# Splitting the second layer's weight slices in a staggered order, and moving conversions and the permutation into the experts

## The chip, the core and the metric

The kernel runs on one core of a Trainium2 chip. Its engines are TensorE (PE; its weight loads are a row of their own, PEld), VectorE (DVE), ScalarE (ACT), GpSimd (POOL) and SyncE (SP), which issues most DMAs. The metric is the device time of one execution in microseconds, a median over runs.

## What is computed

Attention with two sparse masks feeds a mixture of eight experts, one expert per token, and that feeds a second feed-forward layer on all tokens. Cut to what matters here:

```python
x = attention(q, k, v)                       # 2304 tokens of 512
expert_idx = argmax(logits(x, expert_emb))   # one of 8 experts per token
for e in range(8):                           # F = 1024
    h = np.maximum(x[mask] @ w1[e], 0.0)
    out[mask] = gate_w[mask, None] * (h @ w2[e])
h = np.maximum(np.maximum(x @ v1, x @ v2), x @ v3)   # second layer, 768 wide
return h @ v_out
```

All of it is in float32. The kernel keeps that precision by splitting each operand into a rounded high half and the rest (a low half), and multiplies high by high, high by low and low by high: three matmuls for one (`three`, line 818).

## The kernel before

**Stages.** Attention comes first (to some 112 us), then routing, then the experts in order of size (112 to 353 us), then the second layer in three blocks of 768 tokens. In each block `layer1` runs over nine weight slices (numbers 64 to 72) and `layer2` over six groups of 128 tokens.

**Weight slices.** Slices 0 to 63 are the experts' weights, eight for each expert: four for the first product (`gemm1`, two steps f for each slice) and four for the second (`gemm2`, steps d). In the code's tables a step is a pair (e, i): i is f for 0 to 7 and 8 + d after that. Slices 64 to 72 (`UP`) are the second layer's first weights, 73 to 75 its last. A slice is loaded by `w_load` (line 120) into one of three staging tiles, then split by three functions that `w_stages` (line 141) returns: `sums` (line 157, only for `UP`: four VectorE operations that form the combined blocks of the product scheme below, in a small tile `sb`), `upper` (line 162: the high half, on ScalarE, L166) and `rest` (line 168: the low half, on VectorE, L171, then for `UP` the store to `u_scr` for the later blocks, then the next `w_load`). The halves go into a ring of nine tiles; an `UP` slice takes two of them. `freed` (line 191) says which of the ring may be written.

**The planner.** Nothing is scheduled by the compiler: each engine runs its instructions in the order in which the code issues them. The code keeps a clock of its own, `now`, and a time at which its DMA queue is through, `moved` (line 116): each slice load and each conversion load adds 1456, each conversion store 728. `step` (line 263) is called after each product in the experts, moves `now` on, and splits up to two slices if `may_split` (line 259) finds the next one staged for long enough by these clocks and its ring tiles free. `slices(n)` (line 824) forces a split that is still missing when its product comes.

**Conversions.** The second layer's weights come in as 64-bit data and are turned into float32 by 24 conversions. `c_before` (line 219) issues the next load (two buffers) and one conversion: two ScalarE operations, three VectorE ones (L234, L236, L238) and an integer add on GpSimd (L240). `c_store` (line 206) writes the result to `w_scr` two steps later, and only a slice with both its halves stored can be loaded. Before the change 20 of the 24 run in the experts (`c_at_step`, line 1013) and four in `layer1` of block 0 (hook 2, line 1081).

**The permutation.** Rows of the output are written back by an index and scaled by a gate, both made by `perm_step` (line 985): three index steps, four value steps and six parts (VectorE, L892 to L925), and behind each part three small bf16 matmuls (L934) into one PSUM tile of the pool `ps_q`, which has two and also serves the experts' transposes (line 799). Before the change the index and value steps run in experts 2 to 5, the parts in `layer1` of block 0.

**`layer1`.** Each slice of block 0 (line 1084) multiplies by seven products of six matmuls with 384 columns each, in the order A11, S1, (p4 of the slice before), S2, A12, S4, S3. After A11 the sum in PSUM is copied out by ScalarE as a snapshot (L1118) and so are the next two (L1120, L1125), since S2 goes on adding in the same PSUM tile; VectorE then adds the snapshots to later products (`done`, line 1095: L1103, L1105) and takes maxima (L1108, L1101). The last product, p4, is postponed into the next slice. Three hooks (line 1074) in each slice call `up_step` (line 252), which takes one of the three functions of the next slice's split:

```python
if not prep and next_split[0] >= 8 * E and may_split(True):
    prep.extend(w_stages())
if prep:
    prep.pop(0)()
```

So `sums`, `upper` and `rest` of one slice follow each other, and then those of the next one. In the experts `up_step` is called once after each f and twice after each d, and has something to do from expert 7's first `gemm2` on. During experts 5 to 7 and the first slice of block 0, pairs of operations of `x_combos` (line 948: sums L962, then splits L957 on ScalarE and L958 on VectorE) prepare the tokens' side of the products.

Of the kernel before, what the change touches and what calls it, by code (L numbers as in the profile page):

```python
# [20 lines left out]
NT, DM, E, F, F2 = 2304, 512, 8, 1024, 768  # L21
# [48 lines left out]
def kernel(ctx, tc, a, out, x_scr, w_scr, u_scr, perm_scr, gate_scr, upto="all"):  # L70
# [33 lines left out]
    pools = {}  # L104
# [3 lines left out]
    def unit(n):  # L108

        return n + min(max(n - 8 * E, 0), 9)  # L110
    wsl, staged, ev, ready, stored = {}, {}, {}, set(), {}
    next_load, next_split, usable, most_staged = [0], [0], [NA], [M0]
# [24 lines left out]
    def slot_tile(u):  # L137
        i = u % NRING
        return (wp_a if i < NA else pools["wp_b"]).tile([128, 2, 1024], F32R, tag=f"w{i}", name="w")

    def w_stages():

        n = next_split[0]
        next_split[0] += 1
        t = staged.pop(n)[0]
        u, parts, ws = unit(n), [t], []
        if n in UP:

            (a11, a21), (a12, a22) = ([t.rearrange("p (k c g n) -> p k g c n", k=2, c=2, g=2)[:, k, g] for g in range(2)] for k in range(2))
            sb = pools["sb"].tile([128, 3, 256], F32, tag="sb", name="sb")
            s1, s2, s4 = (sb[:, i].rearrange("p (c n) -> p c n", c=2) for i in range(3))
            parts.append(sb.rearrange("p i n -> p (i n)"))

        def sums():
            if n in UP:
                for o, x, y, op in ((s1, a21, a22, ALU.add), (a21, a11, a21, ALU.subtract), (s2, s1, a11, ALU.subtract), (s4, a12, s2, ALU.subtract)):
                    nc.vector.tensor_tensor(out=o, in0=x, in1=y, op=op)  # L160

        def upper():
            for i, x in enumerate(parts):
                m = 1024 - 256 * i
                ws.append(slot_tile(u + i))
                nc.scalar.activation(out=ws[i][:, 0, 0:m], in_=x, func=ACTF.Copy)  # L166

        def rest():
            for i, x in enumerate(parts):
                m = 1024 - 256 * i  # L170
                nc.vector.tensor_tensor(out=ws[i][:, 1, 0:m], in0=x, in1=ws[i][:, 0, 0:m].bitcast(F32), op=ALU.subtract)  # L171
                if n in UP:
                    nc.sync.dma_start(out=u_scr[n - 8 * E, i, :, :, 0:m], in_=ws[i][:, :, 0:m].bitcast(F32))
            wsl[n] = ws if n in UP else ws[0]
            ready.add(n)
            w_load()

        return [sums, upper, rest]
# [34 lines left out]
    def c_after():  # L213

        c_todo[:] = [(k - 1, f) for k, f in c_todo]
        while c_todo and c_todo[0][0] < 0:
            c_todo.pop(0)[1]()
# [29 lines left out]
            c_after()  # L247
            c_before()

    prep = []  # L250

    def up_step():

        if not prep and next_split[0] >= 8 * E and may_split(True):
            prep.extend(w_stages())
        if prep:
            prep.pop(0)()

    def may_split(force=False):
        n = next_split[0]  # L260
        return n in staged and unit(n) + (n in UP) < usable[0] and (force or now[0] >= staged[n][1] + AGE)
# [10 lines left out]
    bctx = ctx.enter_context(ExitStack())  # L272
# [483 lines left out]


    pools["wp_b"] = bctx.enter_context(tc.tile_pool(name="wp_b", bufs=1))
    pools["sb"] = bctx.enter_context(tc.tile_pool(name="sb", bufs=1))
    yt_p = bctx.enter_context(tc.tile_pool(name="yt", bufs=1))  # L760
    xw_p = bctx.enter_context(tc.tile_pool(name="xw", bufs=1))
    xb_p = bctx.enter_context(tc.tile_pool(name="xb", bufs=1))
# [117 lines left out]
    NPT = NTILE // PT  # L880
# [4 lines left out]
    pend_perm, pb = [], {}  # L885
# [99 lines left out]
    def perm_step():  # L985
        if len(pend_perm) > 1 or not perm_todo and pend_perm:
            perm_sum()
        if perm_todo:
            perm_todo.pop(0)()

    perm_todo = [lambda i=i: perm_index(i) for i in range(3)] + [lambda u=u: perm_value(u) for u in range(4)]
# [18 lines left out]

    x_at = {(5, 9): 1, (5, 11): 1, (6, 1): 1, (6, 3): 1, (6, 9): 1, (6, 11): 1}
    x_at.update({(7, 0): 2, (7, 1): 2, (7, 2): 2, (7, 3): 1, (7, 4): 1, (7, 8): 2, (7, 9): 2})
    c_at_step = {(0, 9), (0, 11)} | {(e, i) for e in range(1, 7) for i in (2, 8, 11)}

    def others(e, i):
        for _ in range(x_at.get((e, i), 0)):
            x_todo.pop(0)()
        if len(perm_todo) > NPT and e > 1 and i in (9, 11):
            perm_step()

    for e in range(E):
# [35 lines left out]
    snap = [yt[c][:, NT:NT + HB] for c in range(4)]  # L1057
# [16 lines left out]
    def hook(i):  # L1074


        if i == 0:
            c_after()
        for _ in range(1 if next_split[0] <= UP[-1] + 1 else 2):
            up_step()  # L1080
        if i == 2:
            c_before()

    def layer1(n, first, last, tm, after, early):

        slices(n)
        f = 2 * ((n - 8 * E) // 3)
        fx, fw, fy = (ps_g.tile([128, 512], F32, tag="g", name="g")[:, 0:HB] for i in range(3))
        s1, s5, s2, _ = snap
        tmps = [tm[0][:, 0], tm[0][:, 1], tm[1][:, 0]]  # L1090

        def p(ps, k, x, start):
            product(ps, lambda *z: w_block(n, *z), k, x, start)

        def done(g, half, ps, s, i):
            h = hf[f + g][:, HB * half:HB * half + HB]
            if s is None:
                if first:
                    nc.scalar.activation(out=h, in_=ps, func=ACTF.Copy)
                else:  # L1100
                    nc.vector.tensor_tensor(out=h, in0=ps, in1=h, op=ALU.max)  # L1101
            elif first:
                nc.vector.tensor_tensor(out=h, in0=ps, in1=s, op=ALU.add)  # L1103
            else:
                nc.vector.tensor_tensor(out=tmps[i], in0=ps, in1=s, op=ALU.add)  # L1105
                if i:
                    h, t = (hf[f], tm[0].rearrange("p i n -> p (i n)")) if i == 1 else (h, tmps[2])
                    nc.vector.tensor_tensor(out=h, in0=h, in1=t, op=ALU.max)  # L1108

        def p4():  # L1110
            p(fx, "A22", "T4", False)
            done(1, 0, fx, None, None)
            after()

        while len(x_todo) > 2 and x_now[0]:
            x_todo.pop(0)()
        p(fx, "A11", "B11", True)
        nc.scalar.activation(out=s1, in_=fx, func=ACTF.Copy)  # L1118
        p(fw, "S1", "T1", True)
        nc.scalar.activation(out=s5, in_=fw, func=ACTF.Copy)  # L1120
        while pend:
            pend.pop(0)()
        hook(0)
        p(fx, "S2", "T2", False)
        nc.scalar.activation(out=s2, in_=fx, func=ACTF.Copy)  # L1125
        while x_todo and x_now[0]:
            x_todo.pop(0)()
        hook(1)
        p(fy, "A12", "B21", True)
        done(0, 0, fy, s1, 0)  # L1130

        def p3():
            p(fw, "S4", "B22", False)
            done(0, 1, fw, s2, 1)

        def p7():
            p(fx, "S3", "T3", False)
            done(1, 1, fx, s5, 2)

        for q in (p7, p3) if last else (p3, p7):  # L1140
            q()
        hook(2)
        pend.append(p4)
        if last:
            early()
            pend.pop(0)()
# [12 lines left out]
    def layer2(k, i, fs):  # L1159
        ps = ps_q.tile([128, 512], F32, tag="q", name="q")  # L1160
        for j, f in enumerate(fs):
# [7 lines left out]
        nc.gpsimd.indirect_dma_start(  # L1169
            out=out, out_offset=bass.IndirectOffsetOnAxis(ap=perm_i[:, col:col + 1], axis=0), in_=r, in_offset=None)  # L1170

    units, x_now = {}, [False]
    for k in range(NB):

        order = list(UP)[::-1] if k % 2 else list(UP)
        x_now[0] = k == 0
        if k == 0:
            for f in range(2):
                hf[f] = h_p.tile([128, BLK], F32, tag=f"h{f}", name="hf")
        tm = [h_p.tile([128, 2, HB], F32, tag=f"h{6 + i}", name="tmp") for i in range(2)]  # L1180
        def after(n, j):
            if k == 0:
                freed(n)
                units[n] = unit(n)
            elif j < 6:

                units[order[j + 3]] = units[n]
                up_again(order[j + 3], units[n])

        fs = [4, 5, 2, 3, 0, 1] if k % 2 else [0, 1, 2, 3, 4, 5]  # L1190
        for j, n in enumerate(order):
            layer1(n, j % 3 == 0, j == 8, tm, lambda n=n, j=j: after(n, j), lambda: h_split(0, fs, (0,)))
            if k == 0 and j > 1:
                perm_step()
        while k == 0 and pend_perm:
            perm_step()
        x_todo = x_combos(k + 1) if k + 1 < NB else []
        h_split(0, fs, (1,))
        for i in range(BLK // 128):
            if i + 1 < BLK // 128:  # L1200
                h_split(i + 1, fs)
            layer2(k, i, fs)
            for _ in range(4):
                if x_todo:
                    x_todo.pop(0)()
# [172 lines left out]
```

## Time and profile before

| | us |
|---|---|
| median of 3 runs | 659.03 (656.42 to 660.36) |
| the profiled execution | 656.18 |
| its span, first to last instruction | 654.1 |
| PE busy | 617.3 |
| DVE busy | 456.0 |
| ACT busy | 336.2 |
| POOL busy | 136.8 |

The profiled execution is at the low end of the three runs, and 2.1 us of it lie outside its span. Busy time is a sum over stages with different limits: TensorE is busy for 94% of the span, yet a few per cent of a stage can still be waiting. A matmul's end is modelled, so the distance between starts says more than the busy time. The granted clock is given as a share of full speed (1.00 is 2.4 GHz); a mean between 0.50 and 1.00 over a stretch means that part of it ran at 1.2 GHz.

### The profile page before, as it was taken

The page shows a single profiled execution, that of the slowest core. Times are in us where ns is not written, and L with a number is a line of the kernel's source. Part 1 is how long each engine was busy: PE and PEld are TensorE (multiplying, and loading weights), DVE is VectorE, ACT ScalarE, POOL GpSimd, SP SyncE. Part 2 cuts the span into 40 slices and gives each one's busy share as a digit, 9 for nine tenths or more (in the row PEclk, how much of TensorE's full clock was granted, in tenths as well). Part 3 has the DMA queues.
Part 4 walks back from the last instruction along what each step waited for, and adds up shares of the span by engine and source line. Part 5 has one row for each costly group of instructions (what it writes and reads, how often), then busy time and mean ns, then how long its engine had stood idle before and what let it go on. Part 6 is the DMA issues. An engine that isn't in the chain of part 4 may idle for free.

```text
span 654.1 us, 11928 instructions
## 1 busy us (share of the span) xinstructions
PE 617.3 (94%) x4281; PEld 580.9 (89%) x4282; DVE 456.0 (70%) x1011; ACT 336.2 (51%) x909; POOL 136.8 (21%) x130
## 2 busy tenths in 40 slices
PE   8999998699999999999997878999999999999995
PEld 7888886589999999999997877998999988999974
DVE  5878997587758697879997899977443466334440
ACT  3678877445656566656754544336422246321242
POOL 5434433370413223133100111001100002000011
PEclk9999999899999999999999899899999999999998
DMA  9998661735868697797874987821167401367111
GB/s 226 298 248 231 209 155 51 254 120 184 295 212 289 211 290 255 239 295 243 289 258 156 405 299 261 311 65 49 49 231 263 182 17 65 129 230 262 72 47 53
DMA packets 44880, 130.81 MB, mean 200 GB/s; under 512 B 4632, under 2 KB 15512, under 8 KB 41456
## 3 DMA queue, kind: packets, MB, share of 16 engines
q1 hardware_dynamic: 41792, 120.50, 56.0%
q0 software_dynamic: 3024, 9.49, 4.1%
q8 instruction: 36, 0.59, 0.4%
q14 instruction: 28, 0.23, 0.1%
HBM read 97.73 MB, written 32.24 MB: 199 GB/s over the span
## 4 chain that ended last, share of the span: by engine, by line
PE 74%; DVE 14%; DMA 6%; ACT 2%; issue 2%; SPq 1%; POOL 0%; POOLq 0%; DVEq 0%; ACTq 0%
PE g L821 54%; PE q L821 10%; PE s L373 3%; DVE w L171 3%; DMA qs<-qs 2%; PE x L431 2%; PE r L466 2%; PE q L804 1%; PE t L412 1%; DVE tmp L1105 1%; DMA ql<-ql 1%; DMA stage<-w 1%; DMA out<-r,perm_i 1%; DVE pt L414 1%; DVE off_i L870 1%
## 5 line engine op out<-in xcount | busy, mean ns | idle before, releaser
L821 PE MATMUL g<-xc,w 128*128 128x384 f32 x1134 | 204.6, 341 | 14.0 <-ACT yt L1118 7.3
L821 PEld LDWEIGHTS g<-xc,w 128*128 128x128 f32 x1134 | 200.8, 192 | 16.3 <-ACT yt L1118 8.1
L171 DVE TENSOR_TENSOR w<-stage,w 128x1024 fp32r<-128x1024 f32 x76 | 102.9, 1366 | 21.3 <-ACT w L166 21.3
L821 PE MATMUL g<-h,w 128*128 128x376 f32 (+7 forms) x768 | 111.1, 301 | 0.0
L821 PE MATMUL g<-xw,w 128*128 128x376 f32 (+7 forms) x768 | 105.7, 298 | 1.9 <-DVE w L171 1.4
L821 PEld LDWEIGHTS g<-xw,w 128*128 128x128 f32 x768 | 104.2, 189 | 2.7 <-DVE w L171 1.7
L821 PEld LDWEIGHTS g<-h,w 128*128 128x128 f32 x768 | 104.5, 189 | 0.8
L166 ACT ACTIVATE w<-stage 128x1024 fp32r<-128x1024 f32 x76 | 79.3, 1058 | 37.8 <-DVE stage L160 23.4
L821 PE MATMUL q<-w,hs 128*128 128x512 f32 x324 | 74.9, 391 | 0.9 <-DVE hs L1157 0.8
L821 PEld LDWEIGHTS q<-w,hs 128*128 128x128 f32 x324 | 60.5, 188 | 14.5 <-DVE hs L1157 2.2
L240 POOL TENSOR_TENSOR f<-f,c 128x512 int32<-128x512 int32 x24 | 33.8, 1408 | 165.1 <-DVE f L238 121.6
L1169 POOL DMA_INDIRECT out<-r,perm_i x18 | 17.8, 991 | 228.5 <-ACT r L1168 146.4
L392 ACT ACTIVATE p<-s,nb 128x96 f32<-128x96 f32 (+2 forms) x152 | 50.7, 347 | 22.7 <-DVE r L401 17.6
L1105 DVE TENSOR_TENSOR tmp<-g,yt 128x384 f32<-128x384 f32 x54 | 29.6, 554 | 45.4 <-PE g L821 45.4
L404 POOL TENSOR_TENSOR p<-p,ri 128x384 f32<-128x384 f32 (+3 forms) x44 | 35.9, 816 | 59.4 <-DVE ri L403 43.6
L1118 ACT ACTIVATE yt<-g 128x384 f32<-128x384 f32 x27 | 13.1, 486 | 64.3 <-DVE tmp L1105 32.5
L785 POOL DMA_INDIRECT xg<-x_scr,win_i x22 | 27.0, 1228 | 46.2 <-PE q L804 32.7
L958 DVE TENSOR_TENSOR xc<-yt,xc 128x384 fp32r<-128x384 f32 x42 | 22.2, 571 | 19.5 <-ACT xc L957 19.5
L840 ACT ACTIVATE h<-g 128x376 fp32r<-128x376 f32 (+7 forms) x64 | 25.1, 411 | 19.8 <-PE g L821 17.9
L855 ACT ACTIVATE yt<-g 128x376 f32<-128x376 f32 (+7 forms) x32 | 13.2, 412 | 42.3 <-PE g L821 42.3
L1125 ACT ACTIVATE yt<-g 128x384 f32<-128x384 f32 x27 | 13.3, 491 | 35.3 <-PE g L821 35.3
L414 DVE COPY pt<-t 96x512 f32<-96x512 f32 (+3 forms) x44 | 25.5, 581 | 8.3 <-PE t L412 8.2
(170 smaller groups left out, 814.7 us busy)
## 6 DMA issues: line engine op xcount, KB each, us to landing
stage<-w SPq DMA_DIRECT2D x64, 512.0 KB, 4.8
c<-wm SPq DMA_DIRECT2D x24, 512.0 KB, 6.7
w<-u_scr SPq DMA_DIRECT2D x12, 1024.0 KB, 4.8
u_scr<-w SPq DMA_DIRECT2D x9, 1024.0 KB, 6.2
w<-u_scr SPq DMA_DIRECT2D x12, 768.0 KB, 6.4
u_scr<-w SPq DMA_DIRECT2D x9, 768.0 KB, 6.7
w_scr<-f SPq DMA_DIRECT2D x24, 256.0 KB, 5.3
stage<-w_scr SPq DMA_DIRECT2D x12, 512.0 KB, 7.2
```

Of the source, the lines that this page charges most:

```text
L166: nc.scalar.activation(out=ws[i][:, 0, 0:m], in_=x, func=ACTF.Copy)
L171: nc.vector.tensor_tensor(out=ws[i][:, 1, 0:m], in0=x, in1=ws[i][:, 0, 0:m].bitcast(F32), op=ALU.subtract)
L240: nc.gpsimd.tensor_tensor(out=f, in0=f, in1=low, op=ALU.add)
L373: nc.tensor.matmul(out=ps[:nq, i * nk:(i + 1) * nk], lhsT=q, rhs=k, start=kind == 1, stop=kind == 1 or i == ns - 1, skip_group_check=True)
L392: nc.scalar.activation(out=p[:nq, i, :nk], in_=st[g]["ps"][:nq, i * nk:(i + 1) * nk], func=ACTF.Exp, bias=st[g]["nb"][:nq, i:i + 1], scale ...
L404: nc.gpsimd.tensor_tensor(out=d["p"][:nq, 0:ns, :nk], in0=d["p"][:nq, 0:ns, :nk], in1=ri[:nq, 0:ns].to_broadcast([nq, ns, nk]), op=ALU.mult)
L414: nc.vector.tensor_copy(out=pts[:nk, 0:ns, :nq], in_=pt[:nk, 0:ns * nq].rearrange("p (s q) -> p s q", s=ns))
L785: nc.gpsimd.indirect_dma_start(out=t[i][:r], out_offset=None, in_=x_scr, in_offset=bass.IndirectOffsetOnAxis(ap=win_i[:r, NWIN * e + i:NWI ...
L821: nc.tensor.matmul(out=ps, lhsT=ws(i), rhs=xs(j), start=first and n == 0, stop=last and n == 2, skip_group_check=more)
L840: nc.scalar.activation(out=h[:, 0], in_=ps, func=ACTF.Relu)
L958: nc.vector.tensor_tensor(out=x[:, 1], in0=src[c], in1=x[:, 0].bitcast(F32), op=ALU.subtract)
L1105: nc.vector.tensor_tensor(out=tmps[i], in0=ps, in1=s, op=ALU.add)
```

## The change

Four edits. (1) `up_step` works in rounds of three calls. A round begins, if the next slice can be split, with that slice's `sums`; its other two calls are `upper` and `rest` of the slice whose sums were made one round earlier. The pool of `sb` gets two buffers. Ahead of block 0 the round that is under way is brought to a fixed point. (2) All 24 conversions are issued in the experts, up to step (6, 11), some at other steps than before; hook 2 issues none. (3) The permutation's steps run at listed steps of experts 1 to 5 (`perm_at`), its matmuls included; what might be left is issued ahead of block 0. (4) The first snapshot of a slice alternates between two tiles.

```diff
-    prep = []
+    prep, up_cur = [], [None]
 
     def up_step():
 
-        if not prep and next_split[0] >= 8 * E and may_split(True):
-            prep.extend(w_stages())
-        if prep:
-            prep.pop(0)()
+
+        if not prep:
+            cur, up_cur[0] = up_cur[0], w_stages() if next_split[0] >= 8 * E and may_split(True) else None
+            prep.append(up_cur[0][0] if up_cur[0] else None)
+            prep.extend(cur[1:] if cur else [None, None])
+        f = prep.pop(0)
+        if f:
+            f()
...
-    pools["sb"] = bctx.enter_context(tc.tile_pool(name="sb", bufs=1))
+    pools["sb"] = bctx.enter_context(tc.tile_pool(name="sb", bufs=2))
...
-    c_at_step = {(0, 9), (0, 11)} | {(e, i) for e in range(1, 7) for i in (2, 8, 11)}
+    c_at_step = {(0, 8), (0, 9), (0, 11), (1, 1), (1, 3), (1, 9), (2, 9)} | {(e, i) for e in range(1, 7) for i in (2, 8, 11)} - {(1, 2)}
+    perm_at = {(1, 0), (1, 2), (1, 8), (1, 10), (1, 11), (2, 0), (2, 1), (2, 8), (2, 10), (3, 9), (3, 10), (4, 9), (4, 10), (5, 9), (5, 10)}
...
-        if len(perm_todo) > NPT and e > 1 and i in (9, 11):
+        if (e, i) in perm_at:
             perm_step()
...
             up_step()
-        if i == 2:
-            c_before()
...
-        s1, s5, s2, _ = snap
+        s1, s5, s2 = snap[3 * (n % 2)], snap[1], snap[2]
...
+    while prep and len(prep) != 2:
+        up_step()
+    while perm_todo or pend_perm:
+        perm_step()
...
-            if k == 0 and j > 1:
-                perm_step()
-        while k == 0 and pend_perm:
-            perm_step()
```

## Rows read from the trace of the kernel before

**Rows 1.** Stretches: start:end, us, busy (x count) of PE, PEld, DVE, ACT, POOL, clock, DMA.
```profile
163.00:196.00 33.00, 33.00 (x210) 32.04 (x210) 22.29 (x31) 19.58 (x34) 9.12 (x7) 1.00 0.76 249
196.00:225.00 29.00, 29.00 (x200) 28.30 (x198) 22.67 (x36) 17.37 (x29) 7.29 (x6) 1.00 0.75 254
371.00:381.00 10.00, 8.83 (x51) 8.51 (x51) 9.69 (x15) 5.05 (x9) 2.16 (x1) 1.00 0.99 353
...
352.90:440.50 87.60, 73.57 (x400) 70.61 (x399) 77.95 (x135) 38.13 (x67) 6.69 (x4) 0.92 0.75 273
```

**Rows 2.** TensorE in order of time: start, length, instructions, [idle before, releaser]; block 0, then 1.
```profile
352.94 2.26 PE L821 MATMUL g<-xc,w 128*128 128x384 f32 x12
362.46 15.29 PE L821 MATMUL g<-xc,w 128*128 128x384 f32 x78 [7.26 <-ACT yt L1118]
378.92 7.56 PE L821 MATMUL g<-xc,w 128*128 128x384 f32 x42 [1.17 <-DVE tmp L1105]
388.88 9.12 PE L821 MATMUL g<-xc,w 128*128 128x384 f32 x42 [2.40 <-DVE tmp L1105]
...
408.98 7.09 PE L821 MATMUL g<-xc,w 128*128 128x384 f32 x30 [2.18 <-DVE tmp L1105]
...
416.04 7.54 PE L821 MATMUL g<-xc,w 128*128 128x384 f32 x42
...
464.67 65.92 PE L821 MATMUL g<-xc,w 128*128 128x384 f32 x378
```

**Rows 3.** Waits between 345 and 441 us: who waited for whom, total, times, longest.
```profile
ACT w L166 <- DVE stage L160: 23.4, 9, 3.8
```

**Rows 4.** The chain that ended last, in order of time: start, length, what.
```profile
362.46 8.02 PE g L821 x36
...
423.57 0.14 PE q L934 x3
...
431.21 6.33 PE g L821 x36
```

**Rows 5.** All engines in order of time, block 0: operations beside the add, then one slice's.
```profile
371.79 2.16 POOL L240 TENSOR_TENSOR f<-f,c 128x512 int32<-128x512 int32 x1 [38.27 <-DVE f L238]
372.71 2.05 DVE L171 TENSOR_TENSOR w<-sb,w 128x768 fp32r<-128x768 f32 x1
...
379.38 0.42 DVE L234 TENSOR_SCALAR f<-c 128x512 int32<-128x512 int32 x1
...
380.63 0.69 DVE L238 SCALAR_TENSOR_TENSOR f<-m,f 128x512 f32<-128x512 f32 x1
...
391.79 1.53 DVE L925 TENSOR_TENSOR pb<-pb,val 128x270 bf16<-128x270 bf16 x1
...
410.03 0.43 DVE L925 TENSOR_TENSOR pb<-pb,val 128x270 bf16<-128x270 bf16 x1
410.41 0.56 DVE L1101 TENSOR_TENSOR yt<-g,yt 128x384 f32<-128x384 f32 x1
...
412.02 0.95 DVE L171 TENSOR_TENSOR w<-sb,w 128x768 fp32r<-128x768 f32 x1
...
417.67 0.21 DVE L922 TENSOR_TENSOR pb<-perm_i,cf 128x54 bf16<-128x54 int32 x1
```

**Rows 6.** All engines in order of time: slice 63's split behind expert 7's first gemm2.
```profile
346.49 1.23 DVE L171 TENSOR_TENSOR w<-stage,w 128x1024 fp32r<-128x1024 f32 x1 [3.09 <-ACT w L166]
```

**Rows 7.** Line 133, the load of slice 67, issued at 354.5: issue to landing.
```profile
DMA to landing us min/median/max: 6.8/6.8/6.8
```

**Rows 8.** VectorE in order of time: the first of an index step's six operations.
```profile
252.68 0.20 DVE L892 TENSOR_TENSOR posoh<-oh_all,off_f 128x48 f32<-128x48 bf16 x1
```

**Rows 9.** VectorE and TensorE in order of time: a transpose's split, the next transpose, an early wait.
```profile
298.76 0.40 DVE L797 TENSOR_TENSOR xw<-q,xw 128x248 fp32r<-128x248 f32 x1
299.29 0.38 PE L804 MATMUL q<-cf,xg 128*128 128x128 f32 x2
...
145.28 4.03 PE L821 MATMUL g<-xw,w 128*128 128x376 f32 x22 [1.44 <-DVE w L171]
```

## The prediction

> **What bounds the kernel now.** I read the stretches first, then TensorE's own order of time, then who waited. From 163 to 353 us, the experts, TensorE is busy without a break at a granted clock of 1.00 (2.4 GHz), while VectorE fills 22.3 of 33 us and 22.7 of 29 us of the stretches of experts 1 and 2 [rows 1]. Blocks 1 and 2 of the second layer run the same way: 378 matmuls of 384 columns in 65.9 us [rows 2], or 1.04 us for a product of six and 7.3 us for a slice of seven products. Block 0 does the same 378 matmuls in 87.6 us (352.9 to 440.5), with VectorE busy for 78.0 of them and a mean granted clock of 0.92, so part of it at 1.2 GHz [rows 1]. That is 21 us over block 1, and the only large loss between the attention and the end.
>
> It has two parts. After its first 12 matmuls TensorE stands still for 7.3 us until ScalarE has copied the first sum out (L1118) [rows 2]. After that the slices start 10 us apart (378.9, 388.9, one more, 409.0), and reach 7.5 us only from 416 on [rows 2]. The waits say why: nine times, 23.4 us in all, ScalarE's high half of a weight slice (L166) waits for VectorE's sums (L160), and L1118 stands behind it on ScalarE [rows 3]. The reader is to see two queues taking turns: sums, high half, low half, with the copies that TensorE wants behind them.
>
> **The change, part by part.** The sum goes against the profiled execution (656.2 us, span 654.1); the median shown is 659.0, so I take the difference from that and not from 656.2.
>
> 1. *Slices after the start.* The chain reaches the first postponed product p4 of slice 64 after the 36 matmuls that begin at 362.5, at 370.5, and the last p4 ends at 437.6 [rows 2, 4]: 67.1 us. These are 55 of the 63 products, at 1.04 us 57.2. What takes the difference goes away: four conversions with 1.8 us of VectorE each (three operations from 379.4 to 381.3, 0.42 and twice 0.69), six permutation parts of 1.2 to 2.3 us, and what GpSimd's integer add (L240) does to VectorE beside it: the 768-column subtraction took 2.05 us under one and 0.95 alone, the product L925 1.53 and 0.43 [rows 5]. A slice then leaves VectorE one postponed maximum, two subtractions, four sums, three sums with snapshots and two maxima: from 410.41 to 417.67 that is 7.26 us [rows 5], against 7.28 of TensorE. Every third slice has no maxima and takes some 5.2. With the sums made a round early ScalarE never waits for them. So TensorE should set the pace: −9.9. If staged weights come late the gain shrinks (rival B).
>
> 2. *The start of block 0.* Here the order matters more than the amounts. Conversions made earlier push the planner's time of its DMA queue back (1456 for each load, 728 for each store), so that its weight splits come later: followed through lines 116 to 268, expert 7 now splits 60 (f=1), 61 (f=5) and, behind the first gemm2, 62 and 63, where it split 62 at f=1 and 63 behind that gemm2. The subtraction behind the gemm2 begins at 346.5, since ScalarE's copy of that product's result (L855) comes first [rows 6]. From 346.5 VectorE then has: splits 62 and 63 (2.4), sums of 64 to 67 (4 x 1.6), low halves of 64 and 65 (2 x 2.1), four pairs of activation splits (4.1) and three sums with snapshots (1.5): 18.6, hence 365.1 without a wait. Before, it was one split, four sums, three low halves, and the same rest: 19.5, and with its waits 369.8. The load of 67 is issued behind the stores of 64's two tiles, near 357.5, and such a load took 6.8 us at 354.5 [rows 7]: its sums, which VectorE reaches near 361.5, wait till 364.3, and the pairs and snapshots behind them as long. So p4 of slice 64 comes near 368.5 instead of 370.5: −2. Bounds: −5 (no wait) and +1 (a load of 9 us).
>
> 3. *Permutation products in the experts.* 18 small matmuls, three at a time, 0.14 us on the chain for three [rows 4]: six times, +0.9, where TensorE has no gap. In block 0 they go, which term 1 holds already.
>
> 4. *VectorE, ScalarE and SP in the experts.* Expert 1's stretch gets two more conversions (3.6, and about 0.9 each for the add beside them), three index steps (six small operations of up to 0.20, 1.1 each) and two value steps (0.7) [rows 5, 8]: 22.3 + 3.6 + 1.8 + 3.4 + 0.7 = 31.8 of 33 us. Expert 2 gets one conversion, two parts and two values and gives up two index steps: about 27 of 29. The cover is that weights are split several products ahead of use; it holds while VectorE has any room. On SP the four loads of 0.5 MB and stores of 0.25 MB add 3 MB where the DMA share is 0.75 to 0.76 [rows 1]. A conversion's load waits for the add two conversions earlier, and weight loads stand behind it; with two conversions in neighbouring steps that is one product long. I take +0.5, between 0 and +4.
>
> 5. *One sum buffer for transposes.* The permutation's sums hold one of two PSUM tiles from expert 3 to 5. Transposes then wait for the split of the one before: in expert 5 one such split finished at 299.2 and the next transpose began at 299.3 [rows 9]. Nine such; 0 to +2, taken inside term 4.
>
> 6. *The rest.* The second snapshot buffer removes ScalarE's wait for the sum of the slice before; TensorE has no gap there in blocks 1 and 2, so nothing. Short waits at single slices and some time at 1.2 GHz after the start's two gaps: +1.0, between 0 and +3.
>
> Sum: −9.9 − 2 + 0.9 + 0.5 + 1.0 = −9.5, or **649.5 us** from the median of 659.0.
>
> The add beside VectorE is where a rule speaks against moving conversions: the rows show 1.1 us more for an operation beside one [rows 5]. The Trainium skill, SBUF — State Buffer, section "SBUF: two separate sides", says that VectorE and GpSimd share one port pair as a lock held for a whole instruction, so that the loser stands still. By that each moved conversion would cost the experts up to an add's length; the trace agrees in direction.
>
> **The rivals.**
>
> *B: VectorE and the staged loads still set the pace (18%).* For it: 7.26 us of VectorE against 7.28 leaves no room, and 2.25 MB a slice in 7.3 us is 308 GB/s, where the best row shows 353 at a share of 0.99 [rows 1]. Against: every third slice is light. At 0.8 us more for eight slices, 6.4 of the gain is lost: 656.
>
> *C: the start clears up (12%).* If the load of 67 lands before VectorE wants it, p4 comes at 365.5, the granted clock stays at 1.00 and terms 4 and 6 vanish: −9.9 − 5 + 0.9 = −14: 645.
>
> *D: slower (7%).* VectorE's 31.8 of 33 us in expert 1 is too much. Then splits fall behind their products and TensorE waits for low halves, as it did once for 1.4 us at 145.3 [rows 9]. It decides where the lag passes the lead of some two products, about 8 us; once it does, each of the 16 slices of experts 1 and 2 can cost as much: 22 − 9.5 = +13: 672. Slower needs 13 us of such waits.
>
> *E: the pipeline does nothing (8%).* In-order queues could still leave ScalarE behind VectorE, only the moved work counts: three slices of 10.0 become 7.5, −7.5, +1.4 in the experts: 653.
>
> **How the numbers follow.** The forecast as summed has 55%. About 0.5%, or 3.3 us, is what a measurement of this kernel can tell from no change. Faster: nearly all of the forecast (53), C, E mostly (6) and a third of B (7): 78%. Same: the rest of B mainly, 14%. Slower: D and a slip of B, 8%. The range reaches from C with a better start, 641, to B, 657.
>
> **What would show it.** Right: block 0's matmuls in 74 to 79 us instead of 87.6, slices 7.3 to 7.5 us apart from the third on, almost none of the 23.4 us of L166 behind L160, no L240 or L925 after the experts, and experts ending within 2 us of 353. A gap of TensorE stays at the start, with a wait of L160 for a staged load in it. Wrong: slices of 8 us or more with loads as releasers (B), idle TensorE before 353 (D), or L166 waiting for L160 as before (E).

## The result, and the profile after

The change took 652.33 us in the median (650.87 to 653.97, 4 runs), the kernel before 659.58 beside it (656.42 to 660.36, 4 runs): a ratio of 0.990, 95% interval 0.9854 to 0.9945. Faster by 1.0%, as forecast; but 7.2 us, where 9.5 were summed. The stretch ahead of the first expert product lasts between 130.0 and 135.4 us in the profiled executions of kernels that do the same there, so spans are not compared below; the stretches behind it are.

Busy time by stretch in the kernel after (columns as in [rows 1]): experts 1 and 2, the start of block 0, and block 0 up to layer 2.

```profile
163.00:196.00 33.00, 30.84 (x183) 29.52 (x182) 26.73 (x45) 17.82 (x31) 10.36 (x8) 0.95 0.81 279
196.00:225.00 29.00, 29.00 (x196) 28.30 (x195) 25.68 (x47) 17.53 (x30) 9.26 (x8) 1.00 0.81 275
371.00:381.00 10.00, 5.19 (x21) 4.90 (x20) 7.55 (x15) 1.48 (x3) 0.00 (x0) 0.75 0.89 333
381.00:392.00 11.00, 11.00 (x60) 11.00 (x60) 7.89 (x15) 5.33 (x8) 0.00 (x0) 0.92 0.68 244
362.20:437.70 75.50, 69.08 (x381) 67.84 (x381) 59.73 (x100) 33.96 (x58) 0.00 (x0) 0.95 0.76 282
```

In block 0 VectorE's 78.0 us are down to 59.7 and GpSimd has nothing left [rows 1]. In expert 1 TensorE, busy without a break before, lacks 2.2 of 33 us, and part of that stretch runs at 1.2 GHz (granted clock 0.95).

TensorE in order of time in the kernel after: block 0 and the start of layer 2.

```profile
362.24 0.53 PE L825 MATMUL g<-xc,w 128*128 128x384 f32 x2
364.34 8.30 PE L825 MATMUL g<-xc,w 128*128 128x384 f32 x46 [1.58 <-DVE w L171]
377.44 60.39 PE L825 MATMUL g<-xc,w 128*128 128x384 f32 x330 [4.81 <-DVE hf L1106]
437.67 0.63 PE L825 MATMUL q<-w,hs 128*128 128x512 f32 x2
438.72 24.33 PE L825 MATMUL q<-w,hs 128*128 128x512 f32 x106 [0.42 <-DVE hs L1160]
```

This is the answer to [rows 2]: the slices that began 10 us apart are one run of 330 matmuls, 7.7 us a slice. For the end of the stretch, TensorE in order of time in the kernel before: the last 48 matmuls of `layer1` run to 439.5, and layer 2 follows at 439.7.

```profile
431.04 8.58 PE L821 MATMUL g<-xc,w 128*128 128x384 f32 x48
439.46 0.42 PE L934 MATMUL q<-pb 128*128 128x90 bf16 x6
439.71 25.12 PE L821 MATMUL q<-w,hs 128*128 128x512 f32 x108
```

One gap of 4.8 us is left ahead of the 330, and VectorE's order of time in the kernel after says what it is.

```profile
368.79 1.02 DVE L962 TENSOR_TENSOR xc<-yt,xc 128x384 fp32r<-128x384 f32 x2
373.28 0.43 DVE L160 TENSOR_TENSOR sb<-stage 128x256 f32<-128x256 f32 x1 [3.47 <-DMA stage<-w_scr]
...
375.82 1.48 DVE L1106 TENSOR_TENSOR hf<-g,yt 128x384 f32<-128x384 f32 x3
```

The sums of slice 67 wait 3.5 us for their staged load, and the three sums with snapshots that free TensorE's PSUM tiles stand behind them. The wait of L166 for L160, 23.4 us before [rows 3], isn't in the list any more.

The other side of the ledger is expert 1. From the kernel after, ScalarE, VectorE and TensorE in order of time (three views):

```profile
179.55 0.68 ACT L232 ACTIVATE m<-c 128x512 f32<-128x512 f32 x1 [5.90 <-DMA c<-wm]
...
192.65 0.69 ACT L232 ACTIVATE m<-c 128x512 f32<-128x512 f32 x1 [5.20 <-DMA c<-wm]
```
```profile
185.54 0.20 DVE L896 TENSOR_TENSOR posoh<-oh_all,off_f 128x48 f32<-128x48 bf16 x1
...
186.60 0.43 DVE L234 TENSOR_SCALAR f<-c 128x512 int32<-128x512 int32 x1
...
189.30 1.78 DVE L171 TENSOR_TENSOR w<-stage,w 128x1024 fp32r<-128x1024 f32 x1
191.00 1.32 DVE L845 SCALAR_TENSOR_TENSOR h<-g,h 128x336 fp32r<-128x336 f32 x3
```
```profile
189.03 1.19 PE L825 MATMUL g<-h,w 128*128 128x336 f32 x6 [0.83 <-DVE h L845]
191.55 2.57 PE L825 MATMUL g<-h,w 128*128 128x336 f32 x8 [1.33 <-DVE h L845]
```

ScalarE comes to a conversion before the conversion's load has landed and stands there, 5.9 and 5.2 us. VectorE gets its work late and in one heap (index steps, conversion, low halves, from 182 to 194 without a break), and TensorE waits for the halves of h at the end of it.

By stretches (us; "expert 1" from its first product to expert 2's, "experts 1 to 7" from there to block 0's first product, "block 0" from that to block 1's first, so with layer 2), for all kernels of this study:

| kernel | median, ratio to before [95%] | expert 1 | experts 1 to 7 | block 0 |
|---|---|---|---|---|
| before | 659.6 | 31.9 | 185.9 | 111.7 |
| the change | 652.3, 0.990 [0.9854, 0.9945] | 36.1 | 191.1 | 100.7 |
| pipeline alone (P1) | 674.5, 1.026 [1.0205, 1.0315] | 31.9 | 186.6 | 128.3 |
| pipeline alone, loads in time (Q1) | 657.5, 0.9977 [0.9941, 1.0012] | 31.9 | 186.0 | 110.8 |
| moves alone (P2) | 653.8, 0.994 [0.991, 0.997] | 34.5 | 189.5 | 103.8 |
| change, one snapshot (P3) | 650.0, 0.9907 [0.9873, 0.9942] | 34.4 | 189.1 | 100.6 |
| conversions moved alone (R2) | 652.6, 0.9916 [0.9886, 0.9947] | 33.9 | 188.2 | 104.4 |
| change, permutation left (Q2) | 648.0, 0.9847 [0.9789, 0.9904] | 33.1 | 187.0 | 100.7 |
| change, three conversion buffers (X1) | 645.5, 0.9826 [0.9776, 0.9877] | 32.6 | 187.3 | 99.5 |
| X1, sums two hooks later (S1) | 640.3, 0.9739 [0.968, 0.9797] | 32.2 | 186.9 | 94.1 |
| S1, permutation left (R1) | 639.7, 0.9749 [0.9694, 0.9805] | 31.9 | 185.7 | 95.1 |

So the change gains 11.1 in block 0 and loses 5.2 in the experts in its profiled run, 5.9 together. P2 and P3 have the same order in experts 1 to 6 and lost 3.6 and 3.3, so 5.2 is the high end of what that part costs. All stretches are of one profiled execution each. The expectations count block 0 to where layer 2's matmuls run on without a break; that measure is used where they are compared.

### The profile page after: what moved, and what is told of

The parts are those of the page before. It is cut to its first block, busy times and chain, and to the rows that moved or that the text cites. A ratio compares the mean times of both kernels' runs of the same rounds, so it can differ in the third digit from the quotient of the medians.

```text
span 652.2 us, 11901 instructions
## 1 busy us (share of the span) xinstructions
PE 619.2 (95%) x4281; PEld 582.4 (89%) x4282; DVE 456.8 (70%) x1011; ACT 336.7 (52%) x909; POOL 136.9 (21%) x130
## 4 chain that ended last, share of the span: by engine, by line
PE 74%; DVE 11%; DMA 9%; ACT 2%; issue 2%; SPq 1%; POOL 0%; POOLq 0%; DVEq 0%; ACTq 0%
PE g L825 53%; PE q L825 10%; PE s L377 3%; DMA qs<-qs 2%; PE x L435 2%; DVE w L171 2%; PE r L470 2%; PE t L416 1%; PE q L808 1%; DMA c<-wm 1%; DMA ql<-ql 1%; DMA stage<-w_scr 1%; DMA out<-r,perm_i 1%; DMA w_scr<-f 1%; DVE pt L418 1%
## 5 line engine op out<-in xcount | busy, mean ns | idle before, releaser
L825 PE MATMUL g<-xc,w 128*128 128x384 f32 x1134 | 201.0, 337 | 6.4 <-DVE hf L1106 4.8
L825 PEld LDWEIGHTS g<-xc,w 128*128 128x128 f32 x1134 | 198.8, 190 | 8.3 <-issue 5.1
L171 DVE TENSOR_TENSOR w<-stage,w 128x1024 fp32r<-128x1024 f32 x76 | 106.6, 1414 | 19.5 <-ACT w L166 18.7
L825 PE MATMUL g<-h,w 128*128 128x376 f32 (+7 forms) x768 | 113.0, 303 | 2.2 <-DVE h L845 2.2
L166 ACT ACTIVATE w<-stage 128x1024 fp32r<-128x1024 f32 x76 | 79.3, 1056 | 16.2 <-DMA stage<-w 15.8
L1121 ACT ACTIVATE yt<-g 128x384 f32<-128x384 f32 x27 | 13.3, 492 | 71.7 <-PE g L825 71.7
L844 ACT ACTIVATE h<-g 128x376 fp32r<-128x376 f32 (+7 forms) x64 | 24.7, 415 | 13.3 <-PE g L825 11.2
L396 ACT ACTIVATION_READ_ACCUMULATOR p<-s,nb 128x1 f32 (+2 forms) x152 | 31.1, 204 | 0.0
L232 ACT ACTIVATE m<-c 128x512 f32<-128x512 f32 x24 | 16.3, 680 | 28.4 <-DMA c<-wm 26.0
```

The costliest lines, as they stand in the source:

```text
L396: nc.scalar.activation(out=p[:nq, i, :nk], in_=st[g]["ps"][:nq, i * nk:(i + 1) * nk], func=ACTF.Exp, bias=st[g]["nb"][:nq, i:i + 1], scale ...
L825: nc.tensor.matmul(out=ps, lhsT=ws(i), rhs=xs(j), start=first and n == 0, stop=last and n == 2, skip_group_check=more)
L844: nc.scalar.activation(out=h[:, 0], in_=ps, func=ACTF.Relu)
```

## The experiments

**P1. The pipeline alone.** `up_step` in rounds, two sum buffers and the fixed point ahead of block 0 on the kernel before; conversions, permutation and snapshots as they were.

> The staggered order of the splits alone (two sum buffers; conversions, permutation and snapshots as before). Theory (VectorE's amount of work per slice is the larger part of block 0's loss): the 23 us of ScalarE's high halves behind VectorE's sums go, but a slice with a conversion and a permutation part still holds VectorE for 10 us, so block 0 takes 82 to 87 us instead of 87.6 and the time is 0 to 4 us below that of before; the experts stay at 222.4 us from their first product to block 0's first. Rival (the two queues taking turns is the loss): block 0 takes 76 to 79 us and the time falls by 9 to 11 us.

Neither: block 0 took 103.4 us, 16.6 more than the 86.8 of before. TensorE in order of time in P1, then two rows of its waits between 340 and 465 us (for SyncE between 355 and 462):

```profile
389.67 9.23 PE L825 MATMUL g<-xc,w 128*128 128x384 f32 x42 [7.69 <-ACT yt L1122]
406.90 9.15 PE L825 MATMUL g<-xc,w 128*128 128x384 f32 x42 [8.00 <-ACT yt L1122]
422.30 6.76 PE L825 MATMUL g<-xc,w 128*128 128x384 f32 x24 [6.25 <-ACT yt L1122]
```
```profile
SPq L133 <- DVE w L171: 65.8, 7, 15.3
```
```profile
ACT m L232 <- DMA c<-wm: 30.8, 3, 11.0
```

SyncE stands at L133, the load of a staged slice, until VectorE's L171 has freed its tile; ScalarE stands at L232 for a conversion's load. SyncE in order of time in P1 shows the two next to each other:

```profile
381.69 0.33 SPq L133 DMA_DIRECT2D stage<-w_scr  x1
382.07 0.43 SPq L203 DMA_DIRECT2D c<-wm  x1
```

A slice leaves the count of staged ones when its sums are made, now a round before its tile is free, so the next load is issued a round early and holds SyncE. What is behind it, the conversion's load, leaves only then. (In the change SyncE stands there too, 45.3 us in nine waits between 340 and 470, but no conversion's load is left behind it in block 0.)

**Q1. The same with the loads in time.** This tests that reading: a slice counts as staged until its low halves are made.

```diff
-while n < NSL and len(staged) < most_staged[0] and ...
+while n < NSL and len(staged) + part[0] < most_staged[0] and ...
...
         t = staged.pop(n)[0]
+        part[0] += 1
...
             ready.add(n)
+            part[0] -= 1
             w_load()
```

> The pipeline alone again, but a staged load is issued only when its staging tile has been split: a slice whose sums are made counts as staged until its low halves are made. Theory (why the pipeline alone lost 16 us in block 0): SyncE issues in order, and a staged load issued one round early stood there for its tile (65.8 us of SyncE's L133 behind VectorE's L171, 7 times), with the conversions' loads and stores behind it, and ScalarE waiting for those at L232. Then SyncE's L133 waits fall below 30 us, ScalarE's L232 waits below 6, and block 0 comes from 103.4 to 79 to 86 us (VectorE alone has some 78 us of work there): 650 to 659 us. Rival: the pipeline's order on VectorE itself does it, with conversions and permutation parts between sums and halves: block 0 stays above 95 us, 667 or more.

Block 0 came to 85.9 us and the time to 657.5, both near the slow end of the theory's ranges, and the rival falls. The waits of SyncE, then of ScalarE in Q1:

```profile
SPq L133 <- DVE sb L161: 8.8, 1, 8.8
```
```profile
ACT m L234 <- DMA c<-wm: 13.3, 3, 4.9
```

65.8 us of L133 became 8.8. ScalarE's wait fell from 30.8 to 13.3 and not below 6, so the conversions in block 0 still cost something. SyncE isn't free either: it stands 39.9 us at the stores of the halves (L174), which now come ahead of the load. The early load is the cause of P1's 16.6 us. The pipeline by itself, with the loads in time, is worth some 1.5 us, not told from nothing (0.9941 to 1.0012), and 0.9 us in block 0, although no wait of ScalarE's high halves for VectorE's sums is left in Q1. No run has this bookkeeping together with the moved conversions.

**P2. The moves alone.** The change with the old `up_step`, one sum buffer, one snapshot.

> The moved conversions and the moved permutation alone (old order of the splits, one sum buffer, one snapshot tile). Theory: the experts take 227.7 us as with the whole change, 5.2 more than before; ScalarE still waits for the sums, but the slices are lighter: block 0 takes 78 to 83 us, and the time is 1 to 5 us below that of before. Rival (the pipeline does nothing): block 0 takes 76 to 77 us as with the whole change, and the time is that of the whole change, 6 to 7 us below before.

Block 0 took 79.6 us, 653.8 in all. Between the change and this lie 3.1 us in block 0: what the pipeline adds once the conversions are gone. TensorE in order of time in P2:

```profile
369.74 23.79 PE L821 MATMUL g<-xc,w 128*128 128x384 f32 x120 [7.50 <-ACT yt L1117]
394.04 22.14 PE L821 MATMUL g<-xc,w 128*128 128x384 f32 x126 [0.51 <-DVE tmp L1104]
```

The start's gap is the old one, 7.5 us behind ScalarE's copy; the 10 us slices are gone without the pipeline. L166 still waits for L160, 11.9 us in six, with hardly any of it reaching TensorE (two gaps of 0.5 us above).

**P3. The second snapshot taken back.**

```diff
-        s1, s5, s2 = snap[3 * (n % 2)], snap[1], snap[2]
+        s1, s5, s2, _ = snap
```

> The whole change but for the second snapshot tile (all slices put their first snapshot into one). Theory: TensorE has no gap there, block 0 takes 76.5 us within 1 us and the time is that of the whole change within 1 us. Rival (the snapshot is what ends the waits in block 0): block 0 takes 79 us or more.

Block 0 took 76.47 us, and 76.48 in the change: the second snapshot is worth nothing there. P3 also sets the pipeline against P2, beside the same kernel before and with the same experts but for 0.3 us: 650.0 us against 653.8, and 3.1 us less in block 0.

**R2. The conversions moved alone**, on the kernel before (the new `c_at_step`, no `c_before()` in `hook`).

> The kernel before with one edit: the last four conversions moved into the experts; no pipeline, one sum buffer, the permutation where it was. Theory (the conversions carry nearly all of what the moves gain): block 0 78.5 to 81 us, as with both moves and no pipeline (79.6), and experts 1 to 7 near 187 us (186.97 with the permutation in block 0, 191.1 in the change): 649 to 652.5 us. Rival (without the pipeline the permutation's parts stand between sums and halves and cost what they did): block 0 82 us or more, 653 us or more.

Block 0 took 79.5 us, so the conversions carry 7.3 of the 8.0 that both moves gain there (111.7 to 104.4, and to 103.8). The time, 652.6, and the experts, 188.2, lie a little above what the theory gave.

**Q2. The permutation left in block 0**, the rest as in the change (no `perm_at`; `perm_step()` between the slices as before).

> The change, but with the permutation's parts where they were before (index steps in experts 2 to 6, value parts and products between block 0's slices); the conversions stay moved. Two questions. Expert 1: theory, it lost 4.2 us because ScalarE waits in order for a conversion's load issued too late; then it stays at 34.5 us or more though VectorE loses some 4 us of index and value steps there. Rival: VectorE was overfull, and expert 1 is back near 32 to 33 us. Block 0: six parts of 1.2 to 2.3 us come back to a VectorE that has 7.26 us of work in a slice of 7.28: 5 to 10 us more than 76.5, so 81 to 87. In all 655 to 662 us; if the parts find room after all, block 0 is under 79 and the time about 651.

This missed on both counts. Block 0 stayed at 75.8 us, so moving the permutation gains nothing there, and expert 1 fell to 33.1, near what the rival had. But ScalarE's two long waits are still there. From Q2, ScalarE, then expert 1's stretch (with its clock):

```profile
177.53 0.68 ACT L232 ACTIVATE m<-c 128x512 f32<-128x512 f32 x1 [5.42 <-DMA c<-wm]
...
190.69 0.67 ACT L232 ACTIVATE m<-c 128x512 f32<-128x512 f32 x1 [5.28 <-DMA c<-wm]
```
```profile
169.60:202.70 33.10, 32.21 (x207) 30.97 (x206) 25.68 (x35) 18.09 (x32) 10.75 (x8) 1.00 0.76 259
```

**X1. Three conversion buffers**, the third in the place that holds B21's activations later, so that loads are issued two conversions ahead; permutation moved as in the change.

```diff
-NCV = 2
+NCV = 3
...
-            t = cv_p.tile([128, 1024], I32, tag=f"c{n % NCV}", name="c")
+            t = pools["xb"].tile([128, 1024], I32, tag="xb0", name="c") if n % NCV == 2 else cv_p.tile(...)
...
-        if n:
-
-            c_load()
+        c_load()
```

> The whole change with three buffers for the conversions' input, so that a load is issued two conversions ahead of its use. Theory (expert 1 loses its 4.2 us because conversions two or three steps apart reach ScalarE before their loads have landed, and the activations of the expert stand behind them): the 5.9 and 5.2 us waits of L232 for c<-wm go, expert 1 takes 31.9 to 32.8 us instead of 36.1, and the time is about 4 us below the whole change. Rival (VectorE is overfull in expert 1): expert 1 still takes 35 us or more.

The time was 645.5 us, faster than the kernel before, and than the change without its snapshot beside the same kernel before (P3, 650.0; the runs of the two do not overlap). Expert 1's stretch in X1:

```profile
167.00:199.60 32.60, 32.20 (x206) 30.95 (x205) 30.77 (x55) 20.21 (x35) 9.07 (x7) 1.00 0.79 268
```

VectorE is busy for 30.8 of 32.6 us and TensorE hardly waits; ScalarE has no wait for `c<-wm` left in that stretch. Expert 1 took 31.9 us before, and the runs together say what it lost in the change:

| expert 1 has | runs | us longer than before |
|---|---|---|
| late loads and index steps | the change, P2, P3 | 4.2, 2.6, 2.5 |
| late loads, no index steps | Q2, R2 | 1.2, 2.0 |
| index steps, loads in time | X1, S1 | 0.7, 0.3 |
| neither | R1 | 0.0 |

All of them have two conversions more there than before. So the late load is the larger part, and what the index steps make of a full VectorE the smaller. That the two cost more together than each for itself is not shown: Q2 and R2 have the same order in expert 1 and differ by 0.9 us, and the change's 4.2 holds some 2 us at 1.2 GHz (last section), which P2 and P3 do not have.

**S1. The sums two hooks later**, on X1.

```diff
     while prep and len(prep) != 2:
         up_step()
+    prep[:0] = [None] * 2
```

> Three conversion buffers, and the pipeline's steps two places later in block 0: the sums of slice 67 stand on VectorE behind the sums with snapshots of slice 64 and not ahead of them. Theory: the gap of TensorE at the start of block 0 (4.6 us, VectorE waiting 3.2 us for the staged load of 67 with the sums of products behind it) goes, and the time at 1.2 GHz behind it too: block 0 from 75.3 to 69 to 72 us, 639 to 643 us. Rival: the wait only moves, since the sums of 67 then come late for ScalarE's high half, and TensorE stops at slice 66 or 67 instead: block 0 73.5 us or more, 644 to 648 us.

Block 0 took 69.9 us, and the whole kernel 640.3: what the theory said. TensorE in order of time in S1, then VectorE at the start:

```profile
353.41 0.52 PE L824 MATMUL g<-xc,w 128*128 128x384 f32 x2
355.50 65.79 PE L824 MATMUL g<-xc,w 128*128 128x384 f32 x376 [1.57 <-DVE w L171]
```
```profile
361.82 1.48 DVE L1105 TENSOR_TENSOR hf<-g,yt 128x384 f32<-128x384 f32 x3
364.58 0.42 DVE L160 TENSOR_TENSOR sb<-stage 128x256 f32<-128x256 f32 x1 [1.27 <-DMA stage<-w_scr]
```

The sums with snapshots now stand ahead of the sums of 67. The load still isn't there in time, and its 1.3 us of wait reach nobody. 376 matmuls run in 65.79 us, the pace of block 1 [rows 2]: what X1's block 0 still had over block 1 was for the most part a matter of order. A gap of 1.5 us is left ahead of layer 2's run of 106 matmuls.

**R1. S1 with the permutation left in block 0.**

> Three conversion buffers and the sums two places later, as in the fastest so far (experts 1 to 7 186.9 us, block 0 69.9 us, 640.3 us), but with the permutation's parts back between block 0's slices. Theory (the permutation's parts fit into block 0, since every third slice is light on VectorE and no integer add runs beside them there): block 0 69.5 to 71 us, experts 1 to 7 shorter by 0.5 to 1.5 us since the six groups of products and 4 us of VectorE go from them, 638.5 to 641 us. Rival (with TensorE never waiting and at a clock of 1.00, VectorE's 7.26 us in a slice of 7.28 leaves no room; the parts were hidden before only by the slow start): block 0 72.5 to 77 us, 642 to 647 us.

Block 0 took 70.9 us, the experts were 1.1 us shorter, and the time was 639.7: as the theory had it, and not told from S1. VectorE in order of time in R1, one part of the permutation:

```profile
379.36 0.21 DVE L925 TENSOR_TENSOR pb<-perm_i,cf 128x54 bf16<-128x54 int32 x1
379.48 0.55 DVE L926 TENSOR_TENSOR pb<-z_all,cf 128x384 bf16<-128x384 int32 x1
379.95 0.43 DVE L928 TENSOR_TENSOR pb<-pb,val 128x270 bf16<-128x270 bf16 x1
```

With no integer add beside it a part is 1.2 us, six times, and the light slices hold that: between 366 and 420 VectorE idles only twice, 0.9 and 2.5 us, both in light slices. The four conversions cost the experts nothing here (185.7 against 185.9 us).

## Why the prediction was right, and where it was off

*Term 1, slices after the start (−9.9, with +1.0 of term 6 for the clock): −8.8, in part by luck.* The sum took the end of the last p4 from the chain, 437.6 [rows 4]. The chain leaves TensorE there and follows VectorE; TensorE itself still has 12 matmuls to do and ends at 439.5 (the row of 48 in the section on the result). So from p4 of slice 64 on it was 69.0 us and not 67.1, and it is 60.2 now (377.4 to 437.7). At 57.2, the pace forecast, the gain would have been 11.8. Of the 3.0 us that are missing some 2.7 are the clock, an estimate from the rows of 0.75 and 0.92 (3.6 us at half speed up to 381, and 8% of 11 us): the gap of 4.8 us ahead left TensorE at 1.2 GHz for a while, and term 6 had 1.0 for that. The 1.9 us misread and the 1.7 too few for the clock nearly cancel. S1, without the gap, runs all its 376 at 1.05 us for six.

TensorE set the pace as forecast, but the causes given were wrong in two places. The six permutation parts got a share, and Q2 and R1 show none. And the waits that "say why", ScalarE's high halves behind VectorE's sums, are not what the slices lost: Q1 takes them away and block 0 gains 0.9 us, P2 leaves 11.9 us of them and block 0 gains 8.0. The conversions were most of the loss; the pipeline adds its 3.1 us only once they are gone.

*Term 2, the start (−2): −2.3.* p4 of slice 64 came 15.2 us after block 0's first product instead of 17.5, with the wait of L160 for the load of 67 in it, as written.

*Term 3 (+0.9): held.* Experts 3, 4 and 5 are 0.4, 0.2 and 0.3 us longer, and R1 gets 1.1 back.

*Term 4, the step that failed: +0.5 taken, +2.5 to +4.2 measured in expert 1 (the change and P2, P3), against a range of 0 to +4.* The amount was right: 31.8 us of VectorE forecast, 30.8 in X1. "It holds while VectorE has any room" was the error. VectorE had room, but none behind a wait. The prediction saw that "a conversion's load waits for the add two conversions earlier" and counted only the weight loads behind it; what came late was ScalarE, which stands at L232 in order, and VectorE's work behind it. Of the 4.2 us in the change's own trace 2.2 are two gaps of TensorE, and the rest is the clock behind them. Its sign, experts that end within 2 us of where they did, failed: experts 1 to 7 are 5.2 us longer.

*Terms 5 and 6.* Nothing in the waits speaks of the PSUM buffer; the snapshot is zero, shown by P3.

*Rivals.* D had the place, expert 1, and not the price: 4 us, where slower needed 13. B falls: 330 matmuls run without a gap while VectorE is busy for 59.7 of block 0's 75.5 us. C's clear start came in S1 (block 0 with layer 2 94.1 us instead of 111.7), by another order on VectorE and a third buffer, and not by an earlier load. E's 653 is nearer to the 652.3 measured than the 649.5 forecast, but for another reason: the moves alone are worth about what it said (P2, 653.8), yet the wait of L166 for L160 is gone and the pipeline does add its 3.1 us in block 0. What brings the sum back is the experts, which lost more than E's 1.4.

So block 0 gave 11.1 us where terms 1, 2 and 6 had 10.9, by two errors that cancel, and the experts lost 5.2 us (3.6 and 3.3 in P2 and P3) where terms 3 and 4 had 1.4. The 7.2 us of the medians fall 2.3 short of the sum by term 4.

## What to carry to other kernels

When a buffer is taken earlier in program order, count it as taken until its last reader, or the load issued too soon holds an in-order queue and all behind it (16.6 us in P1). Room on an engine is not enough: ask what stands behind each wait on it, and whether the load ahead is issued early enough (one buffer and two empty steps make the 11 us between the change and S1, 4.2 in the experts and 6.6 in block 0). Work moved off a busy stretch is worth what that stretch lacked: the conversions 7.3 us in block 0, the permutation nothing.

## What the runs showed of the hardware

GpSimd's add beside VectorE, in expert 1 of the change (GpSimd, then VectorE in order of time):

```profile
173.11 1.31 POOL L240 TENSOR_TENSOR f<-f,c 128x512 int32<-128x512 int32 x1 [1.20 <-DMA w_scr<-f]
```
```profile
173.27 2.23 DVE L171 TENSOR_TENSOR w<-stage,w 128x1024 fp32r<-128x1024 f32 x1 [0.30 <-ACT w L166]
...
184.41 1.21 DVE L171 TENSOR_TENSOR w<-stage,w 128x1024 fp32r<-128x1024 f32 x1
```

The subtraction took 2.23 us instead of 1.21, about the 1.15 that the add went on after it had begun (173.27 to 174.42). The Trainium skill, SBUF — State Buffer, section "SBUF: two separate sides", says that a VectorE operation with two inputs in SBUF, as this one has, is blocked for the whole of a GpSimd instruction that reads SBUF and started first; the trace agrees in size (1.02 us longer, 1.15 left of the add). I had not expected that this price could vanish: in R1 the moved adds cost the experts nothing.

The rate of the DMA engines goes higher than the 353 GB/s from which rival B was argued. The start of block 0 in R2, the last column GB/s:

```profile
362.00:372.00 10.00, 6.45 (x22) 6.45 (x23) 7.28 (x15) 5.96 (x11) 0.00 (x0) 0.53 1.01 408
```

The same row has the clock: behind a gap of 7.5 us it was 0.53, behind 4.8 us in the change 0.75 and 0.92. Behind 1.6 us in S1 it stayed at 1.00:

```profile
353.40:363.00 9.60, 8.03 (x47) 7.66 (x46) 9.50 (x17) 5.30 (x11) 0.00 (x0) 1.00 0.70 233
```

Yet gaps as short went both ways. In expert 1 of the change the 8 matmuls behind gaps of 0.8 and 1.3 us took 2.57 us and the clock between 192 and 194 was 0.50; in P2, behind gaps of 0.7 and 1.3 us, the same 8 took 1.50 us at 1.00. TensorE in order of time in P2:

```profile
187.33 1.20 PE L821 MATMUL g<-h,w 128*128 128x336 f32 x6 [0.72 <-DVE h L841]
189.85 1.50 PE L821 MATMUL g<-h,w 128*128 128x336 f32 x8 [1.32 <-DVE h L841]
```
